# Token-major hashing with the bits in the split tile, in an attention and FFN kernel on one core

## The chip, the cores and the metric

The kernel runs on one core of one Trainium2 chip. The metric is the time of the kernel on the device in microseconds (us). Executions of the kernel before agree within 0.6% in four runs. The rounds ran on different chips. Each run has a state: "slow" if it took over 1.5% more than the fastest run of the same kernel.

TensorE has a clock that is granted to it, full or half.

## The reference, cut to what matters

Attention with a hash mask for 4 batches, 8 heads, 768 tokens and 64 dimensions a head, then an FFN with a maximum of three products:

```python
q_bits = (einsum('bhsd,dk->bhsk', q, proj) > 0)      # 6 bits; k_bits in the same way
mask = q_bucket[:, :, :, None] == k_bucket[:, :, None, :]
scores = where(mask, q @ k^T / 8, -1e9)
attn = softmax(scores);  x = (attn @ v) as [3072, 512]
h = maximum(maximum(x @ w1, x @ w2), x @ w3)
out = h @ w_out
```

## The kernel before

q and k are scaled and split into a high fp16 part (64 columns) and a rest (64 columns), in a tile `s` with tokens on the partitions, and transposed into `T`. The score matmul contracts 70 rows: 64 dimensions and 6 rows of hash bits, scaled so large that tokens of different buckets get no weight. Two heads form a pair, and half a sequence (384 tokens) of a pair is a block. A *unit* is one score tile of 256 keys by 384 queries: two score matmuls, one exponential on ScalarE, six attend matmuls two units later. There are 192 units, 12 per pair. The program is one hand-written order of steps, one step per unit; FFN matmul groups ("atoms") are strewn between the units once the first half of batch 0 is done.

The hash in the old kernel works on the transposed tile (bits by rows), with all tokens as moving columns, and writes the bits of each head into rows 64 to 69 of `T`:

```python
def hash_mm(sets):                          # 16 matmuls of 384 columns a pair
    for m, (i, w) in enumerate(ws):
        for g, (t, hh, half) in enumerate(sets[i]):
            nc.tensor.matmul(hps[32*g : 32*(g+1), 0:HQ], w[:], t[:, a : a + CH, :], ...)

def prep(b, pr, s):                         # batches 2 and 3, pr = 0..3
    ...                                     # (the high parts)
    at_end(s + 1, lambda: split_r("q", b, pr)); at_end(s + 1, lambda: xbar("q", b, pr))
    at_end(s + 3, lambda: split_r("k", b, pr)); at_end(s + 3, lambda: xbar("k", b, pr))
    tail(b, pr, s + 12)                     # the hash

for b in range(1, B):                       # (the steps of one pair; the next pair comes at s + 11)
        at(s - 8, lambda: load_pair(b, pr, nc.sync))
        (front if b == 1 else prep)(b, pr, s)
        at(s + 4, lambda: vcast(b, pr)); at(s + 9, lambda: meanv(b, pr), 0.34)
```

`xbar` is a transpose by DMA, put into the queue of SP, which also carries the loads of q, k, v and the outputs. (A transfer is *issued* when SP hands it over; it has *landed* when the profile shows its completion.) Batches 0 and 1 transpose on TensorE (`front`). Pairs follow each other by 11 steps, the loads of a pair go into the queue at step `s - 8`, and what stands in `at_end` goes in at the *end* of its step.

The softmax here doesn't subtract the row's maximum and nothing guards it: scores larger than these inputs give would overflow.

## Time and profile before

| | before |
|---|---|
| median time | 307.63 us (306.75 to 308.55, 4 runs) |
| span of the profile, mean granted clock | 306.0 us, 0.974 |
| score of unit 0, 35, 60, 132 starts at (TensorE's timeline) | 8.8, 56.8, 97.2, 200.2 us |
| first FFN matmul | 63.9 us |

How long a matmul really takes is read from start to next start in TensorE's timeline (start, length, what, and how many of them):

```profile
start us, us, engine line op out<-in xcount [idle before <-releaser]
190.77 0.49 PE L265 MATMUL sc<-qT,kT 70*128 70x384 f16 x2
191.10 0.35 PE L285 MATMUL av<-vone,AT 128*128 128x65 f16 x6
191.28 0.81 PE L329 MATMUL ps<-xT,w_sb 128*128 128x384 f16 x4
191.93 0.49 PE L265 MATMUL sc<-qT,kT 70*128 70x384 f16 x2
```

Two scores take 0.33 us (190.77 to 191.10), six attends 0.18 us, an FFN group 0.65 us.

What TensorE waits for most is VectorE (columns: us in all, times, longest):

```profile
PE tps L162 <- DVE qs L152: 11.9, 7, 4.3
```

### The profile page before, as it was taken

The numbers are of one execution on the slowest core, as the hardware profiler recorded it, in microseconds if no ns is written. First come the engines' busy times: TensorE is split into PE (matmuls) and PEld (weight loads), VectorE is DVE, ScalarE is ACT, GpSimd is POOL, SyncE is SP. The second block draws the span as 40 slices with busy tenths as digits, with TensorE's granted clock in tenths as the row PEclk, the third lists the DMA queues.
The fourth block names the chain that finished last, engine by engine and source line by source line (L and its number), as shares of the span: only waits on it lengthen the run. The fifth ranks groups of instructions, "written<-read, shape, count | busy, mean of one in ns | idle before, by whom it ended". The sixth has DMA issues, their size and how long they took to land.

```text
span 306.0 us, 7090 instructions
## 1 busy us (share of the span) xinstructions
PE 276.1 (90%) x2896; PEld 176.6 (58%) x2896; DVE 212.0 (69%) x455; ACT 200.6 (66%) x265; POOL 9.3 (3%) x17
## 2 busy tenths in 40 slices
PE   3847888989969989999999989999999999999994
PEld 1444565656646656565666556656666665666551
DVE  5687996877995867969587677969664454455551
ACT  3425658968646667777778676868676787786220
POOL 1370000000000000000000000000000000000000
PEclk9969979999997999999999999999999999999998
DMA  7999940006326285915809490926002001100202
GB/s 216 372 287 264 227 131 2 3 5 185 132 56 172 45 233 130 222 39 113 249 15 230 114 246 20 237 95 136 2 1 105 2 0 54 53 1 2 103 0 104
DMA packets 46080, 35.20 MB, mean 115 GB/s; under 512 B 26656, under 2 KB 42976, under 8 KB 46048
## 3 DMA queue, kind: packets, MB, share of 16 engines
q1 hardware_dynamic: 42016, 31.61, 37.7%
q0 software_dynamic: 3952, 3.15, 6.5%
q8 instruction: 22, 0.36, 0.5%
q14 instruction: 10, 0.08, 0.1%
q10 hardware_dynamic: 80, 0.00, 0.0%
HBM read 25.17 MB, written 6.29 MB: 103 GB/s over the span
## 4 chain that ended last, share of the span: by engine, by line
PE 74%; DVE 18%; ACT 3%; issue 2%; DMA 1%; SPq 0%; DVEq 0%; ACTq 0%
PE ps L329 28%; PE sc L265 16%; PE av L285 9%; PE po L341 9%; PE hps L179 4%; PE tps L162 4%; DVE qs L152 3%; ACT AT L269 2%; DVE hb L184 2%; DVE ks L146 2%; DVE ks L152 2%; PE xps L315 2%; DVE kT L188 2%; PE svp L244 1%; DVE t L301 1%
## 5 line engine op out<-in xcount | busy, mean ns | idle before, releaser
L269 ACT ACTIVATE AT<-sc,bias_t 128x768 f16<-128x768 f32 x192 | 169.1, 902 | 73.2 <-PE sc L265 72.7
L329 PE MATMUL ps<-xT,w_sb 128*128 128x384 f16 x576 | 112.4, 327 | 1.9 <-DVE ht L336 1.7
L265 PE MATMUL sc<-qT,kT 70*128 70x384 f16 x384 | 96.4, 332 | 4.2 <-ACT AT L269 1.6
L285 PEld LDWEIGHTS <-AT 128*128 128x128 f16 x1152 | 61.3, 98 | 31.1 <-issue 6.9
L336 DVE TENSOR_TENSOR ht<-ht,ps 128x384 f16<-128x384 f16 x96 | 52.9, 552 | 34.4 <-PE ps L329 31.6
L285 PE MATMUL av<-vone,AT 128*128 128x65 f16 x1152 | 67.1, 193 | 4.4 <-DVE t L301 4.3
L329 PEld LDWEIGHTS <-w_sb 128*128 128x128 f16 x576 | 50.8, 98 | 30.9 <-issue 5.8
L265 PEld LDWEIGHTS <-kT 70*128 70x128 f16 x384 | 34.0, 100 | 23.9 <-issue 6.4
L341 PE MATMUL po<-wout_sb,ht 128*128 128x512 f16 x144 | 34.8, 379 | 0.0
L334 ACT CAST ht<-ps 128x384 f16<-128x384 f32 x48 | 22.8, 474 | 16.3 <-PE ps L329 16.1
L301 DVE TENSOR_TENSOR t<-av,mv 128x390 f32<-128x390 f32 x32 | 17.9, 560 | 10.1 <-PE av L285 10.0
L184 DVE TENSOR_SCALAR hb<-hps 128x384 f16<-128x384 f32 x28 | 15.2, 553 | 8.7 <-PE hps L179 8.6
L162 PE MATMUL tps<-iden,qs 128*128 128x128 f16 x96 | 9.7, 259 | 12.7 <-DVE qs L152 11.9
L341 PEld LDWEIGHTS <-ht 128*128 128x128 f16 x144 | 12.8, 97 | 13.1 <-issue 0.6
L347 DVE COPY osb<-po 128x512 f32<-128x512 f32 x16 | 11.0, 688 | 11.5 <-PE po L341 11.5
L305 DVE TENSOR_TENSOR xn<-t,rr 128x384 f16<-128x384 f32 x32 | 17.9, 558 | 1.1
L152 DVE SCALAR_TENSOR_TENSOR qs<-q,qs 128x768 f16<-128x768 f32 (+1 forms) x17 | 16.5, 972 | 0.1
L162 PEld LDWEIGHTS <-qs 128*128 128x128 f16 x96 | 7.4, 116 | 14.7 <-DVE qs L152 13.3
L316 DVE COPY xT<-xps 128x384 f16<-128x384 f16 x32 | 11.3, 353 | 6.2 <-PE xps L315 5.9
L152 DVE SCALAR_TENSOR_TENSOR ks<-k,ks 128x768 f16<-128x768 f32 (+1 forms) x17 | 15.3, 906 | 0.3
L179 PE MATMUL hps<-kT,PA 128*32 128x384 f16 x64 | 11.1, 343 | 1.0 <-DVE kT L170 0.9
L170 DVE COPY kT<-tps 128x768 f16<-128x768 f16 x16 | 8.6, 553 | 4.3 <-PE tps L162 4.2
(43 smaller groups left out, 172.9 us busy)
## 6 DMA issues: line engine op xcount, KB each, us to landing
v<-in_v_dram SPq DMA_DIRECT2D x16, 384.0 KB
out_dram<-osb SPq DMA_DIRECT2D x24, 256.0 KB
q<-in_q_dram SPq DMA_DIRECT2D x15, 384.0 KB
k<-in_k_dram SPq DMA_DIRECT2D x15, 384.0 KB
w_sb<-in_moe_w_dram POOLq DMA_DIRECT2D x6, 384.0 KB, 13.3
wout_sb<-in_moe_w_out_dram POOLq DMA_DIRECT2D x1, 768.0 KB, 22.0
q<-in_q_dram SPq DMA_DIRECT2D x2, 192.0 KB
k<-in_k_dram SPq DMA_DIRECT2D x2, 192.0 KB
```

Of the source, the lines that this page charges most:

```text
L152: nc.vector.scalar_tensor_tensor(out=s[:, a, D : 2 * D], in0=x32, scalar=QS, in1=s[:, a, 0:D], op0=AluOp.mult, op1=AluOp.subtract)
L162: nc.tensor.transpose(p16[:, c * P : (c + 1) * P], S16[n, b, pr][:, hh * NCH + c, :], iden[:])
L179: nc.tensor.matmul(hps[32 * g : 32 * (g + 1), 0:HQ], w[:], t[:, a : a + CH, :], start=m == 0, stop=m == len(ws) - 1)
L184: nc.vector.tensor_scalar(out=out, in0=hps[:, 0:HQ], scalar1=0.0, scalar2=0.5, op0=AluOp.is_gt, op1=AluOp.subtract)
L265: nc.tensor.matmul(sc[:, i, 0:HQ], kT[0:KR, hh * NCH + 2 * j + i, :], qT[0:KR, hh * NCH + hf * CH : hh * NCH + (hf + 1) * CH, :], start=Tr ...
L269: nc.scalar.activation(AT[:], sc[:, :, 0:HQ], ActFn.Exp, bias=bias_t[:], scale=EXP_SCALE)
L285: nc.tensor.matmul(av[:, o : o + D + 1], AT[:, i, c * P : (c + 1) * P], vones[b % 2][:, 2 * pr + hh, 2 * j + i, 0 : D + 1], start=first, s ...
L301: nc.vector.tensor_tensor(out=t[:, :, :, 0 : D + 1], in0=av[:, :, :, 0 : D + 1], in1=mvs[b, pr][:].unsqueeze(2).to_broadcast([P, 2, CH, D ...
L329: nc.tensor.matmul(ps[:, 0:HQ], w_sb[i][:, jc, fb * P : (fb + 1) * P], xT[:, jc, :], start=jc == 0, stop=jc == NJ - 1)
L334: nc.scalar.copy(ht[:], ps[:, 0:HQ])
L336: nc.vector.tensor_tensor(out=hts[fb][:], in0=hts[fb][:], in1=ps[:, 0:HQ], op=AluOp.max)
L341: nc.tensor.matmul(ps[:], hts[fb][:, c * P : (c + 1) * P], wout_sb[:, fb, :], start=fb == 0, stop=fb == NF - 1)
```

## The change

The intent is to unload TensorE and VectorE. The hash becomes 24 matmuls of 12 columns a pair, with the transposed tokens as weights, so that the bits come out with tokens on the partitions. Three small VectorE operations write them into the split tile, over the rest part (which is not needed once the hash is made), and the tile is *transposed a second time*: now rows 64 to 69 of `T` hold the bits. x is transposed by DMA. V is summed on GpSimd, so that the mean of V takes one matmul, not six. In batch 0 half 0 of all pairs comes before half 1 of pair 1, so that the FFN can start after 35 units instead of 41. The start gets 32 matmuls to warm TensorE. Two more changes are not in the cut below: the preparation of a pair starts two steps earlier in batches 2 and 3 (three in batch 1), and the exponential takes its bias as a constant and no longer from a tile. The core of the diff (cuts marked):

```diff
+    def hash_bits(b, pr, heads=(0, 2)):
+        ... for n, hh, c:
+            nc.tensor.matmul(hps[:, a*2*NBITS : (a+1)*2*NBITS], T[b, pr][:, a, :], PAB[:], start=True, stop=True)
+        ... neg = -hps[6:12];  bit = hps[0:6] > neg;  s[:, :, D : D+NBITS] = (bit - 0.5) * 2*BIT
+    def T2(b, pr, s, by_pe):
+        at(s, lambda: hash_bits(b, pr), 0.7)
+        if by_pe: ... second transposes on TensorE (pairs 0 and 1 of batch 0)
+        else:
+            at_end(s, lambda: xbar("q", b, pr))
+            at_end(s, lambda: xbar("k", b, pr))
     def prep(b, pr, s):
         ... (first transposes by DMA, as before)
-        tail(b, pr, s + 12)
+        T2(b, pr, s + 9, False)
-    blocks = [... ((0, 0), (0, 1), (1, 0), (1, 1), (2, 0), (3, 0), (2, 1), (3, 1))]
+    blocks = [... ((0, 0), (0, 1), (1, 0), (2, 0), (3, 0), (1, 1), (2, 1), (3, 1))]
-            at(u + LAG + 3, lambda: x_T(b, hf, pr), 0.2)
+            ... first and last half: x_T as before; all others:
+                at(u + LAG + 2, lambda: x_bar(b, hf, pr))
+                if pr == NP - 1: at(u + LAG + 6, lambda: push_ffn(...))
+        nc.gpsimd.tensor_tensor(...)  x3   # V's sums, into one of two buffers vsums[pr % 2]
-            at(s + 9, lambda b=b, pr=pr: meanv(b, pr), 0.34)
+            at(s + 9, lambda b=b, pr=pr: meanv(b, pr), 0.06)
-    begin = 6 * NUP + 5
+    begin = 5 * NUP + 5
```

More of the change, by code (lines that the diff above doesn't have):

```diff
@@ L48 @@
     EPS = 1e-30
+    NA = 2 * 2 * NCH
+    NA2 = 2 * NCH
+    WARM = 32
     konst = ctx.enter_context(tc.tile_pool(name="konst", bufs=1))
     raw = ctx.enter_context(tc.tile_pool(name="raw", bufs=4))
-    spl = ctx.enter_context(tc.tile_pool(name="spl", bufs=3))
+    spl = ctx.enter_context(tc.tile_pool(name="spl", bufs=4))
     opnd = ctx.enter_context(tc.tile_pool(name="opnd", bufs=8))
@@ L88 @@
         load(n, 0, 1, nc.sync)
-    bias_t = konst.tile([P, 1], FP32, name="bias_t")
-    nc.vector.memset(bias_t[:], EXP_BIAS)
     warm = konst.tile([P, 1], FP32, name="warm")
-    nc.scalar.activation(warm[:], bias_t[:], ActFn.Exp)
+    nc.vector.memset(warm[:], 0.0)
+    nc.scalar.activation(warm[:], warm[:], ActFn.Exp)
+    ones = konst.tile([P, P], FP16, name="ones")
+    nc.vector.memset(ones[:], 1.0)
     iden = konst.tile([P, P], FP16, name="iden")
     make_identity(nc, iden[:])
-    ones = konst.tile([P, P], FP16, name="ones")
-    nc.vector.memset(ones[:], 1.0)
+    wps = mm_ps.tile([P, 512], FP32, tag="mm", name="wps")
+    for _ in range(WARM):
+        nc.tensor.matmul(wps[:, 0:P], ones[:], ones[:], start=True, stop=True)
+    vsums = []
+    for i in range(2):
+        t = konst.tile([P, 2, D + 1], FP16, name=f"vsum{i}", tag=f"vsum{i}")
+        nc.vector.memset(t[:, :, D : D + 1], float(NCH))
+        vsums.append(t)
     vones = []
@@ L102, with make_p @@
         vones.append(t)
-    ph = konst.tile([D, NBITS], FP16, name="ph")
-    pr32 = konst.tile([D, NBITS], FP32, name="pr32")
-    PA, PB = [], []
-    for i in range(2):
-        for n, l in (("PA", PA), ("PB", PB)):
-            l.append(konst.tile([P, 32], FP16, name=f"{n}{i}", tag=f"{n}{i}"))
-            nc.vector.memset(l[i][:], 0.0)
-    def make_p(i):
-        if i == 0:
-            nc.vector.tensor_copy(ph[:], p32[:])
-            nc.vector.tensor_tensor(out=pr32[:], in0=p32[:], in1=ph[:], op=AluOp.subtract)
+    PAB = konst.tile([P, 2 * NBITS], FP16, name="PAB")
+    def make_p():
+        ph = konst.tile([D, NBITS], FP16, name="ph")
+        pr32 = konst.tile([D, NBITS], FP32, name="pr32")
+        nc.vector.tensor_copy(ph[:], p32[:])
+        nc.vector.tensor_tensor(out=pr32[:], in0=p32[:], in1=ph[:], op=AluOp.subtract)
         for o in (0, D):
-            for l, src in ((PA, ph), (PB, pr32)):
-                nc.vector.tensor_scalar(out=l[i][o : o + D, NBITS * i : NBITS * (i + 1)], in0=src[:],
+            for i, src in enumerate((ph, pr32)):
+                nc.vector.tensor_scalar(out=PAB[o : o + D, NBITS * i : NBITS * (i + 1)], in0=src[:],
                                         scalar1=1024.0, scalar2=None, op0=AluOp.mult)
@@ L134, in operands, with chunks, raw_view @@
     def operands(b, pr):
-        for n in "qk":
-            S16[n, b, pr] = spl.tile([P, 2 * NCH, 2 * D], FP16, tag=n + "s", name=n + "s")
-            T[n, b, pr] = opnd.tile([P, 2 * NCH, P], FP16, tag=n + "T", name=n + "T")
+        S16[b, pr] = spl.tile([P, NA, 2 * D], FP16, tag="s", name="s")
+        T[b, pr] = opnd.tile([P, NA, P], FP16, tag="T", name="T")
+    def chunks(n, heads=(0, 2)):
+        o = NA2 * "qk".index(n)
+        return o + heads[0] * NCH, o + heads[1] * NCH
+    def raw_view(n, b, pr, heads):
+        return raws[n, b, pr][:].rearrange("p h (c d) -> p (h c) d", d=D)[:, heads[0] * NCH : heads[1] * NCH, :]
     def split_h(n, b, pr, eng, heads=(0, 2)):
-        a = slice(heads[0] * NCH, heads[1] * NCH)
-        x32 = raws[n, b, pr][:].rearrange("p h (c d) -> p (h c) d", d=D)[:, a, :]
-        o = S16[n, b, pr][:, a, 0:D]
+        a0, a1 = chunks(n, heads)
+        o = S16[b, pr][:, a0:a1, 0:D]
+        x32 = raw_view(n, b, pr, heads)
         if eng is nc.scalar:
@@ L148, in split_r @@
     def split_r(n, b, pr, heads=(0, 2)):
-        a = slice(heads[0] * NCH, heads[1] * NCH)
-        x32 = raws[n, b, pr][:].rearrange("p h (c d) -> p (h c) d", d=D)[:, a, :]
-        s = S16[n, b, pr]
-        nc.vector.scalar_tensor_tensor(out=s[:, a, D : 2 * D], in0=x32, scalar=QS,
-                                       in1=s[:, a, 0:D], op0=AluOp.mult, op1=AluOp.subtract)
+        a0, a1 = chunks(n, heads)
+        s = S16[b, pr]
+        nc.vector.scalar_tensor_tensor(out=s[:, a0:a1, D : 2 * D], in0=raw_view(n, b, pr, heads), scalar=QS,
+                                       in1=s[:, a0:a1, 0:D], op0=AluOp.mult, op1=AluOp.subtract)
     def xbar(n, b, pr):
-        nc.sync.dma_start_transpose(T[n, b, pr][:], S16[n, b, pr][:].rearrange("p a d -> p (a d)"))
+        a0, a1 = chunks(n)
+        nc.sync.dma_start_transpose(T[b, pr][:, a0:a1, :], S16[b, pr][:, a0:a1, :].rearrange("p a d -> p (a d)"))
     def pe_T(n, b, pr, hh):
@@ L160, in pe_T, with evac_T @@
         p16 = ps[:].bitcast(FP16)
+        a0, a1 = chunks(n, (hh, hh + 1))
         for c in range(NCH):
-            nc.tensor.transpose(p16[:, c * P : (c + 1) * P], S16[n, b, pr][:, hh * NCH + c, :], iden[:])
+            nc.tensor.transpose(p16[:, c * P : (c + 1) * P], S16[b, pr][:, a0 + c, :], iden[:])
         return p16
-    def evac_T(p16, n, b, pr, hh, eng, c0=0, c1=NCH):
-        o = T[n, b, pr][:, hh * NCH + c0 : hh * NCH + c1, :].rearrange("p a t -> p (a t)")
+    def evac_T(p16, n, b, pr, hh, eng):
+        a0, a1 = chunks(n, (hh, hh + 1))
+        o = T[b, pr][:, a0:a1, :].rearrange("p a t -> p (a t)")
@@ L167, in evac_T @@
         if eng is nc.scalar:
-            nc.scalar.copy(o, p16[:, c0 * P : c1 * P])
+            nc.scalar.copy(o, p16[:, 0 : NCH * P])
         else:
-            nc.vector.tensor_copy(o, p16[:, c0 * P : c1 * P])
-    def hash_mm(sets):
+            nc.vector.tensor_copy(o, p16[:, 0 : NCH * P])
+    def hash_bits(b, pr, heads=(0, 2)):
         hps = mm_ps.tile([P, 512], FP32, tag="mm", name="hps")
-        ws = [(i, l[i]) for l in (PA, PB) for i in range(len(sets))]
-        for m, (i, w) in enumerate(ws):
-            for g, (t, hh, half) in enumerate(sets[i]):
-                a = hh * NCH + half * CH
-                nc.tensor.matmul(hps[32 * g : 32 * (g + 1), 0:HQ], w[:], t[:, a : a + CH, :],
-                                 start=m == 0, stop=m == len(ws) - 1)
-        return hps
@@ L183, in hash_cmp @@
-    def hash_cmp(out, hps):
-        nc.vector.tensor_scalar(out=out, in0=hps[:, 0:HQ], scalar1=0.0, scalar2=0.5,
-                                op0=AluOp.is_gt, op1=AluOp.subtract)
-    def hash_row(dst, src):
-        nc.vector.tensor_scalar(out=dst, in0=src, scalar1=2 * BIT, scalar2=None, op0=AluOp.mult)
-    hbs = {}
-    def hash_pair(b, pr):
-        hb = small.tile([P, HQ], FP16, tag="hb", name="hb")
-        hbs[b, pr] = hb
-        g = [(T[n, b, pr], hh) for hh in range(2) for n in "qk"]
-        hash_cmp(hb[:], hash_mm([[(t, hh, half) for t, hh in g] for half in range(2)]))
-        hash_row(hb[:], hb[:])
@@ L199, in hash_half @@
-    def hash_half(b, pr, half):
-        if half == 0:
-            hbs[b, pr] = small.tile([P, S], FP16, tag="hb2", name="hb2")
-        g = [(T[n, b, pr], hh, half) for hh in range(2) for n in "qk"]
-        hash_cmp(hbs[b, pr][:, half * HQ : (half + 1) * HQ], hash_mm([g]))
-    def hash_head_rows(b, pr, hh):
-        for i, n in enumerate("qk"):
-            dst = T[n, b, pr][D : D + NBITS, hh * NCH : (hh + 1) * NCH, :].rearrange("p a t -> p (a t)")
-            o = 32 * (2 * hh + i)
-            hash_row(dst, hbs[b, pr][o : o + NBITS, :])
@@ L211, in hash_rows @@
-    def hash_rows(b, pr):
-        hb = hbs.pop((b, pr))
-        for g, (n, hh) in enumerate((("q", 0), ("k", 0), ("q", 1), ("k", 1))):
-            for half in range(2):
-                a = hh * NCH + half * CH
-                o = 32 * g + NBITS * half
-                nc.sync.dma_start(T[n, b, pr][D : D + NBITS, a : a + CH, :].rearrange("p a t -> p (a t)"),
-                                  hb[o : o + NBITS, :])
-    def hash_head(b, pr, hh):
-        tq, tk = T["q", b, pr], T["k", b, pr]
-        hb = small.tile([P, HQ], FP16, tag="hb", name="hb")
-        hash_cmp(hb[:], hash_mm([[(tk, hh, 0), (tq, hh, 0), (tk, hh, 1), (tq, hh, 1)]]))
-        for g, (t, half) in enumerate(((tk, 0), (tq, 0), (tk, 1), (tq, 1))):
-            a = hh * NCH + half * CH
-            hash_row(t[D : D + NBITS, a : a + CH, :].rearrange("p a t -> p (a t)"),
-                     hb[32 * g : 32 * g + NBITS, :])
+        for n in range(2):
+            for hh in range(*heads):
+                for c in range(NCH):
+                    a = n * NA2 + hh * NCH + c
+                    nc.tensor.matmul(hps[:, a * 2 * NBITS : (a + 1) * 2 * NBITS], T[b, pr][:, a, :], PAB[:],
+                                     start=True, stop=True)
@@ new lines, in hash_bits @@
+        bit = small.tile([P, 2, 2 * NCH, NBITS], FP16, tag="bit", name="bit")
+        hv = hps[:, 0 : NA * 2 * NBITS].rearrange("p (n a k) -> p n a k", n=2, k=2 * NBITS)
+        sl = slice(heads[0] * NCH, heads[1] * NCH)
+        neg = small.tile([P, 2, 2 * NCH, NBITS], FP32, tag="neg", name="neg")
+        nc.vector.tensor_scalar(out=neg[:, :, sl, :], in0=hv[:, :, sl, NBITS : 2 * NBITS], scalar1=-1.0,
+                                scalar2=None, op0=AluOp.mult)
+        nc.vector.tensor_tensor(out=bit[:, :, sl, :], in0=hv[:, :, sl, 0:NBITS], in1=neg[:, :, sl, :],
+                                op=AluOp.is_gt)
@@ L230, in vcast @@
+        s4 = S16[b, pr][:].rearrange("p (n a) d -> p n a d", n=2)
+        nc.vector.tensor_scalar(out=s4[:, :, sl, D : D + NBITS], in0=bit[:, :, sl, :], scalar1=0.5,
+                                scalar2=2 * BIT, op0=AluOp.subtract, op1=AluOp.mult)
+    mvs = {}
     def vcast(b, pr):
-        v32 = raws.pop(("v", b, pr))[:].rearrange("p h (c d) -> p h c d", d=D)
+        v32 = raws.pop(("v", b, pr))
         o = vones[b % 2][:, 2 * pr : 2 * pr + 2, :, 0:D]
+        src = v32[:].rearrange("p h (c d) -> p h c d", d=D)
@@ L233, in vcast @@
         if b == 0:
-            nc.gpsimd.tensor_copy(o, v32)
-        else:
-            nc.scalar.copy(o, v32)
-    mvs = {}
+            nc.gpsimd.tensor_copy(o, src)
+            return
+        nc.scalar.copy(o, src)
+        half = CH * D
+        t = small.tile([P, 2, half], FP32, tag="vt", name="vt")
+        nc.gpsimd.tensor_tensor(out=t[:], in0=v32[:, :, 0:half], in1=v32[:, :, half : 2 * half], op=AluOp.add)
+        t2 = small.tile([P, 2, D], FP32, tag="vt2", name="vt2")
+        nc.gpsimd.tensor_tensor(out=t2[:], in0=t[:, :, 0:D], in1=t[:, :, D : 2 * D], op=AluOp.add)
@@ L240, in meanv @@
+        nc.gpsimd.tensor_tensor(out=vsums[pr % 2][:, :, 0:D], in0=t2[:], in1=t[:, :, 2 * D : 3 * D], op=AluOp.add)
     def meanv(b, pr):
         ps = mm_ps.tile([P, 512], FP32, tag="mm", name="svp")
-        for c in range(NCH):
-            nc.tensor.matmul(ps[:, 0 : 2 * (D + 1)].rearrange("p (h d) -> p h d", h=2), ones[:],
-                             vones[b % 2][:, 2 * pr : 2 * pr + 2, c, 0 : D + 1], start=c == 0, stop=c == NCH - 1)
+        o = ps[:, 0 : 2 * (D + 1)].rearrange("p (h d) -> p h d", h=2)
@@ L246, in meanv @@
+        if b == 0:
+            for c in range(NCH):
+                nc.tensor.matmul(o, ones[:], vones[0][:, 2 * pr : 2 * pr + 2, c, 0 : D + 1],
+                                 start=c == 0, stop=c == NCH - 1)
+        else:
+            nc.tensor.matmul(o, ones[:], vsums[pr % 2][:], start=True, stop=True)
         mv = vpool.tile([P, 2, D + 1], FP32, tag=f"mv{pr}", name="mv")
@@ L252 @@
     NU = NCH // 2
-    blocks = [(0, hf, pr) for pr, hf in ((0, 0), (0, 1), (1, 0), (1, 1), (2, 0), (3, 0), (2, 1), (3, 1))]
+    blocks = [(0, hf, pr) for pr, hf in ((0, 0), (0, 1), (1, 0), (2, 0), (3, 0), (1, 1), (2, 1), (3, 1))]
     blocks += [(b, hf, pr) for b in range(1, B) for hf in range(2) for pr in range(NP)]
@@ L262, in score @@
         sc = sc_ps.tile([P, 2, 512], FP32, tag="sc", name="sc")
-        qT, kT = T["q", b, pr], T["k", b, pr]
+        qkT = T[b, pr]
         for i in range(2):
-            nc.tensor.matmul(sc[:, i, 0:HQ], kT[0:KR, hh * NCH + 2 * j + i, :],
-                             qT[0:KR, hh * NCH + hf * CH : hh * NCH + (hf + 1) * CH, :],
+            nc.tensor.matmul(sc[:, i, 0:HQ], qkT[0:KR, NA2 + hh * NCH + 2 * j + i, :],
+                             qkT[0:KR, hh * NCH + hf * CH : hh * NCH + (hf + 1) * CH, :],
                              start=True, stop=True)
         AT = atp.tile([P, 2, HQ], FP16, tag="AT", name="AT")
-        nc.scalar.activation(AT[:], sc[:, :, 0:HQ], ActFn.Exp, bias=bias_t[:], scale=EXP_SCALE)
+        nc.scalar.activation(AT[:], sc[:, :, 0:HQ], ActFn.Exp, bias=EXP_BIAS, scale=EXP_SCALE)
         ATs[u] = AT
@@ L289, in attend @@
             norm(b, hf, pr)
-            at(u + LAG + 3, lambda: x_T(b, hf, pr), 0.2)
+            if (b, hf) in ((0, 0), (B - 1, 1)):
+                at(u + LAG + 3, lambda: x_T(b, hf, pr), 0.2)
+            else:
+                at(u + LAG + 2, lambda: x_bar(b, hf, pr))
+                if pr == NP - 1:
+                    at(u + LAG + 6, lambda: push_ffn(b, hf, xTs.pop((b, hf))))
     xTs = {}
@@ L306, in norm, with x_tile, x_bar, x_T @@
                                 op=AluOp.mult)
-    def x_T(b, hf, pr):
+    def x_tile(b, hf):
         if (b, hf) not in xTs:
             xTs[b, hf] = xp.tile([P, NJ, HQ], FP16, tag="xT", name="xT")
+        return xTs[b, hf]
+    def x_bar(b, hf, pr):
+        o = x_tile(b, hf)[:, pr, :].rearrange("p (c t) -> p c t", c=CH)
+        nc.sync.dma_start_transpose(o, xns.pop((b, hf, pr))[:].rearrange("p c d -> p (c d)"))
+    def x_T(b, hf, pr):
+        x_tile(b, hf)
         xn = xns.pop((b, hf, pr))
@@ L368, in at_end, with tr, pair_T @@
         todo_end.setdefault(step, []).append(fn)
+    def tr(n, b, pr, hh, eng=nc.vector):
+        evac_T(pe_T(n, b, pr, hh), n, b, pr, hh, eng)
+    def pair_T(b, pr, hh, eng):
+        pq = pe_T("q", b, pr, hh)
+        pk = pe_T("k", b, pr, hh)
+        evac_T(pq, "q", b, pr, hh, nc.vector)
+        evac_T(pk, "k", b, pr, hh, eng)
     operands(0, 0)
@@ L375 @@
     split_r("k", 0, 0, (0, 1))
-    make_p(0)
-    pq = pe_T("q", 0, 0, 0)
-    pk = pe_T("k", 0, 0, 0)
-    evac_T(pq, "q", 0, 0, 0, nc.vector)
-    evac_T(pk, "k", 0, 0, 0, nc.vector)
+    pair_T(0, 0, 0, nc.scalar)
+    make_p()
     split_h("q", 0, 0, nc.scalar, (1, 2))
     split_h("k", 0, 0, nc.scalar, (1, 2))
+    hash_bits(0, 0, (0, 1))
+    pair_T(0, 0, 0, nc.scalar)
     split_r("q", 0, 0, (1, 2))
-    hash_head(0, 0, 0)
     split_r("k", 0, 0, (1, 2))
@@ L388, in first_b @@
     def first_b():
-        pq = pe_T("q", 0, 0, 1)
-        pk = pe_T("k", 0, 0, 1)
-        evac_T(pq, "q", 0, 0, 1, nc.vector)
-        evac_T(pk, "k", 0, 0, 1, nc.vector)
+        pair_T(0, 0, 1, nc.vector)
+        hash_bits(0, 0, (1, 2))
+        pair_T(0, 0, 1, nc.vector)
     at(1, first_b)
-    at(2, lambda: hash_head(0, 0, 1))
     def load_pair(b, pr, eng):
@@ L399, in load_pair, with front @@
             load(n, b, pr, eng)
-    def front(b, pr, s):
+    def T2(b, pr, s, by_pe):
+        at(s, lambda: hash_bits(b, pr), 0.7)
+        if by_pe:
+            at(s + 1, lambda: pair_T(b, pr, 0, nc.vector), 0.7)
+            at(s + 2, lambda: pair_T(b, pr, 1, nc.vector), 0.7)
+        else:
+            at_end(s, lambda: xbar("q", b, pr))
+            at_end(s, lambda: xbar("k", b, pr))
+    def front(b, pr, s, by_pe=False):
         at(s, lambda: operands(b, pr))
@@ L407, in front @@
         at_end(s + 1, lambda: split_r("k", b, pr))
-        def tr(n, hh):
-            evac_T(pe_T(n, b, pr, hh), n, b, pr, hh, nc.vector)
+        k = 2 if b == 0 else 1
         for i, (n, hh) in enumerate((("q", 0), ("q", 1), ("k", 0), ("k", 1))):
-            at(s + 2 + i // (2 if b == 0 else 1), lambda n=n, hh=hh: tr(n, hh), 0.34)
-        tail(b, pr, s + (4 if b == 0 else 7))
-    def tail(b, pr, s):
-        if b == 1:
-            at(s, lambda: hash_pair(b, pr), 0.67)
-            at(s, lambda: hash_rows(b, pr))
-        else:
-            at(s, lambda: hash_half(b, pr, 0), 0.34)
-            at(s + (b > 0), lambda: hash_half(b, pr, 1), 0.34)
-            for hh in range(2):
-                at_end(s + (b > 0) * (1 + hh), lambda hh=hh: hash_head_rows(b, pr, hh))
-    at(0, lambda: vcast(0, 1))
-    at(0, lambda: load_pair(0, 2, nc.sync))
-    at(2, lambda: make_p(1))
-    front(0, 1, 2)
-    at(2, lambda: meanv(0, 0), 0.34)
-    at(3, lambda: load_pair(0, 3, nc.sync))
-    at(6, lambda: vcast(0, 2))
-    for i in range(3):
-        at(7 + i, lambda i=i: load_w(i, 0))
-        at(15 + i, lambda i=i: load_w(i, 1))
-    front(0, 2, 11)
-    at(10, lambda: meanv(0, 1), 0.34)
-    at(15, lambda: vcast(0, 3))
-    front(0, 3, 18)
-    at(20, lambda: meanv(0, 2), 0.34)
-    at(26, lambda: meanv(0, 3), 0.34)
-    at(18, lambda: nc.gpsimd.dma_start(wout_sb[:], moe_w_out.rearrange("(c p) m -> p c m", p=P)))
+            at(s + 2 + i // k, lambda n=n, hh=hh: tr(n, b, pr, hh), 0.34)
+        T2(b, pr, s + 2 + 4 // k, by_pe)
     def prep(b, pr, s):
@@ L451, in prep @@
         at_end(s + 3, lambda: xbar("k", b, pr))
-        tail(b, pr, s + 12)
+        T2(b, pr, s + 9, False)
+    at(0, lambda: vcast(0, 1))
+    at(0, lambda: load_pair(0, 2, nc.sync))
+    at(1, lambda: load_pair(0, 3, nc.sync))
+    front(0, 1, 2, True)
+    at(3, lambda: meanv(0, 0), 0.34)
+    at(5, lambda: vcast(0, 2))
+    for i in range(3):
+        at(4 + i, lambda i=i: load_w(i, 0))
+        at(9 + i, lambda i=i: load_w(i, 1))
+    front(0, 2, 8)
+    at(10, lambda: meanv(0, 1), 0.34)
+    at(12, lambda: vcast(0, 3))
+    front(0, 3, 13)
+    at(17, lambda: meanv(0, 2), 0.34)
+    at(22, lambda: meanv(0, 3), 0.34)
+    at(16, lambda: nc.gpsimd.dma_start(wout_sb[:], moe_w_out.rearrange("(c p) m -> p c m", p=P)))
     for b in range(1, B):
         for pr in range(NP):
-            s = 33 + 7 * pr if b == 1 else 2 * (b - 1) * NUG + 4 + 11 * pr
+            s = 30 + 7 * pr if b == 1 else 2 * (b - 1) * NUG + 2 + 11 * pr
             at(s - 8, lambda b=b, pr=pr: load_pair(b, pr, nc.sync))
```

## The prediction

> **What bounds the kernel now.** From about 100 us to the end, TensorE: in the table of busy time by stretches of 10 us, PE is busy 9.2 to 10.0 of 10 us from 100 to 300 us, and VectorE falls to 5 to 7. From 10 to 60 us it is the preparation of the first pairs on VectorE (busy 7 to 9 of 10 us) together with the chains PE-VectorE-PE of hashing; ScalarE's exponentials, 192 of 0.90 us, wait for scores there (in the timeline score unit 5 runs at 21.9, unit 23 at 47.7, unit 41 at 64 us: 1.3 us a unit where the exponential needs 0.85). The FFN starts at 63.9 us. The last 20 us are a TensorE tail (FFN of the last half) and an output DMA, and don't change.
>
> **TensorE's real cost, by start-to-start times in PE's timeline (190 to 200 us).** Two scores 0.33, six attends 0.18 (30 ns each), an FFN group 0.65, an output group 1.29, three x transposes 0.17, six mean-V matmuls 0.35, hashing half a pair about 0.45 with its gaps (0.85 a pair). Sum about 259 us, so 47 us are idle or throttled: 4 at the start, 4 to 5 at the end, most of the rest before 130 us.
>
> **What the change does on TensorE.** Hashing becomes 24 matmuls of 12 columns with 128-column weights. At the attend rate of 30 ns they take 0.7 us a pair: little saved, about 0.15 x 16 = 2.4 us. (The Trainium skill, "TensorE: Matmul & The Clock Gate", Back-to-back issue gap, gives about 25 ns as the floor for small matmuls; the 30 ns agree roughly.) Mean V: 12 x 0.29 = 3.5 us saved. x transposes to DMA: 24 x 0.17 = 4.1 us saved. Second transposes of two pairs: 2.7 us added, where TensorE is idle anyway. So about 10 us leave the TensorE-bound part, all critical.
>
> **VectorE.** Hash compare and rows, 2.5 us a pair, become three small operations, about 0.7 us. 24 evictions of 0.35 us go. Pairs 0 and 1 get four more evictions of 0.55 us each. Before the FFN VectorE has some 5 us less, but the start chain is longer: a second transpose round, make_p behind the first eviction; +1 us to the first score, +2 us for head 1.
>
> **Order.** The FFN can start after 35 units instead of 41. With 1.3 us a unit and less VectorE work I expect its first matmul at 57 us instead of 63.9. That lets 157 instead of 151 units be mixed with FFN.
>
> **DMA.** A 384 KB transpose takes some 3.3 us from issue, 2 us of it at 210 GB/s (stretches of 0.5 us at 206 to 210 us; the skill, "DMA: Bandwidth & Descriptors", Latency and other measured facts, states 261 GB/s, the trace shows less). Second transposes in steady state have slack; pair 2 and 3 of batch 0 have 6 to 7 units, beside weight loads: 1 to 3 us of stall. The eight small row DMAs a pair of batch 1 (0.73 us of issue each) go.
>
> **Sum.** 57 + 218 (TensorE work left) + 10 (stalls, 12 now) + 4.5 (end) = 290 us; I say 291. Range 284 to 299. Chances: faster 0.87, same 0.11, slower 0.02.
>
> **Right or wrong if the profile shows:** FFN's first matmul at 54 to 60 us; hash matmuls 25 to 32 ns apart; TensorE 10 of 10 us from 110 us on; VectorE busy down by 25 to 30 us in all.
>
> **What would make it wrong:** transposes queueing behind loads and output on SP, so that FFN groups or scores wait for xT or T; GpSimd's sums slowing VectorE (weight issues stretch a 0.95 us operation to 2.09 at 17.6 us); hash matmuls limited by weight loads at 60 ns or more.

## More of the kernel before

From the page of the kernel before: busy time of TensorE, then busy tenths of TensorE in 40 slices of the span, its granted clock, and the busy share of the 16 DMA engines.

```profile
PE 276.1 (90%) x2896; PEld 176.6 (58%) x2896; DVE 212.0 (69%) x455; ACT 200.6 (66%) x265; POOL 9.3 (3%) x17
...
PE   3847888989969989999999989999999999999994
...
PEclk9969979999997999999999999999999999999998
DMA  7999940006326285915809490926002001100202
```

The next view gives busy time of each engine in three stretches, and at the end of each line the granted clock, the DMA share and GB/s.

```profile
core 0: us, PE busy (x) PEld busy (x) DVE busy (x) ACT busy (x) POOL busy (x), PEclk, DMA share, GB/s
96.00:126.00 30.00, 28.99 (x326) 18.20 (x324) 22.43 (x48) 21.61 (x29) 0.00 (x0) 1.00 0.60 147
126.00:160.00 34.00, 33.55 (x351) 20.78 (x349) 25.68 (x56) 25.60 (x34) 0.00 (x0) 1.00 0.47 126
160.00:210.00 50.00, 48.94 (x513) 30.31 (x511) 37.64 (x79) 37.11 (x51) 0.00 (x0) 1.00 0.71 159
```

From 126 us TensorE is busy all the time, and the DMA engines 0.47 to 0.71 of it.

The queue of SP around one k transpose looks like this (start, time of issue, what):

```profile
122.47 1.43 SPq L156 DMA_TRANSPOSE qT<-qs  x1
123.95 0.89 SPq L78 DMA_DIRECT2D q<-in_q_dram  x1
124.89 0.47 SPq L78 DMA_DIRECT2D k<-in_k_dram  x1
125.41 0.47 SPq L78 DMA_DIRECT2D v<-in_v_dram  x1
126.30 1.69 SPq L156 DMA_TRANSPOSE kT<-ks  x1
```

The k transpose is issued behind the three loads of the next pair. The loads cost it no time in the queue here: VectorE's last operation on its data ended at 126.3 us too. Its hash comes nine steps later, and no wait of TensorE for a transpose by DMA stands in the list of waits.

## The result, and the profile after

The changed kernel took 328.38 us in the median (325.75 to 330.95, 4 runs), against 307.63. The ratio is 1.063 (1.055 to 1.071). Ratios here and below are the mean time of one kernel's fast runs over that of the other's in the same rounds, so they are not quite the ratio of the medians quoted. The profiled run, 330.95 us, counts as slow; the three fast ones had a clock of 0.909 to 0.911, the profiled one 0.895.

The same lines of the page, after:

```profile
PE 288.7 (88%) x2972; PEld 190.8 (58%) x2972; DVE 191.5 (58%) x398; ACT 189.1 (57%) x267; POOL 35.3 (11%) x53
...
PE   6697797979779885959999995979999999999795
...
PEclk9559876789997997896999997895999999999999
DMA  7999469658569997585895987598563003001102
```

TensorE's row has holes, the clock row has many more low digits, and the DMA row is fuller. By stretches, with the columns as before:

```profile
96.00:126.00 30.00, 23.38 (x266) 15.43 (x265) 18.78 (x38) 16.86 (x24) 5.36 (x8) 0.94 1.04 224
126.00:160.00 34.00, 29.53 (x257) 17.64 (x258) 17.24 (x36) 17.22 (x25) 2.74 (x5) 0.80 0.67 147
160.00:210.00 50.00, 46.02 (x485) 29.72 (x483) 27.93 (x60) 32.85 (x48) 5.72 (x9) 0.93 0.86 189
```

From 96 to 126 us the DMA share is 1.04, against 0.60 (packets count where they start, so a share can come out slightly above 1; I read it as: the engines are full). TensorE's clock falls to 0.80 from 126 to 160 us. The waits of TensorE name what it stands for:

```profile
engine line waited for: us in total, times, longest us
PE hps L190 <- DMA T<-s: 12.9, 5, 4.6
PE tps L173 <- DVE s L161: 5.8, 6, 1.9
...
PE sc L250 <- DMA T<-s: 1.9, 1, 1.9
```

The hash matmuls, of which none waited for the DMA before, wait 12.9 us. For a second transpose a score waits only once, before unit 24, the first of pair 3 of batch 0 (at 51.7 us). One of the stops at the hash, in TensorE's timeline:

```profile
121.94 0.45 PE L190 MATMUL hps<-PAB,T 128*128 128x12 f16 x12
126.95 0.49 PE L190 MATMUL hps<-PAB,T 128*128 128x12 f16 x12 [4.56 <-DMA T<-s]
127.29 0.27 PE L230 MATMUL svp<-vsum,ones 128*128 128x130 f16 x1
127.35 0.84 PE L250 MATMUL sc<-T 70*128 70x384 f16 x2
127.99 0.54 PE L270 MATMUL av<-vone,AT 128*128 128x65 f16 x6
```

The hash of q runs at 121.94, and that of k has to wait 4.56 us for its first transpose. Then the same two scores take 0.64 us (127.35 to 127.99) that took 0.33: half clock. Why the transpose is late stands in the queue of SP:

```profile
117.29 1.39 SPq L305 DMA_TRANSPOSE xT<-xn  x1
118.73 0.59 SPq L81 DMA_DIRECT2D q<-in_q_dram  x1
119.36 0.47 SPq L81 DMA_DIRECT2D k<-in_k_dram  x1
119.92 0.41 SPq L81 DMA_DIRECT2D v<-in_v_dram  x1
120.44 0.41 SPq L347 DMA_DIRECT2D out_dram<-osb  x1
120.94 3.34 SPq L166 DMA_TRANSPOSE T<-s  x1
```

The data of this k transpose were complete at 116.7 us (the end of VectorE's rest operation of k in the trace). The queue first issued an x transpose, the three loads of the next pair (1.2 MB) and an output; the k transpose was issued at 120.94, 4.2 us late, and landed at 126.9, behind the loads, which landed at 122.7 to 124.8.

To see where the time went, each matmul's time to the next matmul's start was compared with the usual spacing of its form at full clock. What was more is "idle" where TensorE had ended for over 0.1 us, and "half clock" where the granted clock was half; this is worked out from the traces, and is good to perhaps 1 us. "Half clock" in us is thus what it cost, and not how long it lasted. The first column is the time to unit 60, then follow units 60 to 132 with their idle and half-clock parts, and the rest.

| profile | to unit 60 | units 60 to 132 | of it idle | of it half clock | unit 132 to end |
|---|---|---|---|---|---|
| before | 97.2 | 103.0 | 2.5 | 0.0 | 105.7 |
| changed | 108.2 | 119.2 | 14.0 | 11.2 | 101.8 |
| changed, loads behind (e9 below) | 100.9 | 101.9 | 5.3 | 2.7 | 102.5 |
| same, later hash, old order (e10 below) | 102.2 | 96.5 | 1.4 | 0.0 | 103.5 |

The stretches don't hold quite the same FFN work: up to unit 60 the old kernel does 14 FFN groups of 0.65 us, e10 15, and the changed kernel and e9, with the new order, 18; from unit 132 it is 72, 70, 69 and 69, and the last three have two output groups of 1.29 us less there. So a first or last column is comparable between the kernels only to within 2 to 5 us. And up to step 42 the changed kernel and e9 are the same program: most of the 7.3 us between their first columns is the start, which varies from run to run (unit 35 came at 57.3 to 64.4 us with the same instructions).

### The profile page after: what moved, and what is told of

It is laid out like the page before. It is cut to its first block, busy times and chain, and to the rows that moved or that the text cites. A ratio compares the mean times of both kernels' runs of the same rounds, so it can differ in the third digit from the quotient of the medians.

```text
span 329.2 us, 7303 instructions
## 1 busy us (share of the span) xinstructions
PE 288.7 (88%) x2972; PEld 190.8 (58%) x2972; DVE 191.5 (58%) x398; ACT 189.1 (57%) x267; POOL 35.3 (11%) x53
## 4 chain that ended last, share of the span: by engine, by line
PE 66%; DVE 15%; DMA 13%; ACT 2%; issue 2%; SPq 1%; ACTq 0%; DVEq 0%
PE ps L327 27%; PE sc L250 15%; DMA T<-s 11%; PE av L270 8%; PE po L339 8%; PE tps L173 4%; DVE s L161 4%; PE hps L190 2%; DVE s L156 2%; ACT AT L254 2%; DMA xT<-xn 2%; DVE T L182 1%; DVE ht L334 1%; DVE xn L295 1%; DVE t L291 1%
## 5 line engine op out<-in xcount | busy, mean ns | idle before, releaser
L254 ACT ACTIVATE AT<-sc 128x768 f16<-128x768 f32 x192 | 153.0, 811 | 99.6 <-PE sc L250 97.7
L250 PE MATMUL sc<-T 70*128 70x384 f16 x384 | 104.8, 358 | 3.6 <-DMA T<-s 1.9
L270 PEld LDWEIGHTS <-AT 128*128 128x128 f16 x1152 | 66.0, 103 | 34.9 <-issue 12.9
L250 PEld LDWEIGHTS <-T 70*128 70x128 f16 x384 | 35.0, 105 | 21.4 <-issue 4.5
L173 PE MATMUL tps<-iden,s 128*128 128x128 f16 x240 | 24.2, 262 | 9.9 <-DVE s L161 5.8
L216 POOL TENSOR_TENSOR vt<-v 128x384 f32<-128x384 f32 x12 | 11.9, 995 | 154.4 <-DMA v<-in_v_dram 154.4
L182 DVE COPY T<-tps 128x768 f16<-128x768 f16 x38 | 20.3, 552 | 10.7 <-PE tps L173 10.2
L190 PE MATMUL hps<-PAB,T 128*128 128x12 f16 x384 | 13.5, 170 | 14.8 <-DMA T<-s 12.9
L173 PEld LDWEIGHTS <-s 128*128 128x128 f16 x240 | 19.1, 120 | 12.9 <-DVE s L161 7.9
L190 PEld LDWEIGHTS <-T 128*128 128x128 f16 x384 | 11.9, 98 | 16.3 <-DMA T<-s 13.4
L161 DVE SCALAR_TENSOR_TENSOR s<-q,s 128x768 f16<-128x768 f32 (+1 forms) x17 | 17.0, 1004 | 0.2
```

The costliest lines, as they stand in the source:

```text
L161: nc.vector.scalar_tensor_tensor(out=s[:, a0:a1, D : 2 * D], in0=raw_view(n, b, pr, heads), scalar=QS, in1=s[:, a0:a1, 0:D], op0=AluOp.mul ...
L173: nc.tensor.transpose(p16[:, c * P : (c + 1) * P], S16[b, pr][:, a0 + c, :], iden[:])
L182: nc.vector.tensor_copy(o, p16[:, 0 : NCH * P])
L190: nc.tensor.matmul(hps[:, a * 2 * NBITS : (a + 1) * 2 * NBITS], T[b, pr][:, a, :], PAB[:], start=True, stop=True)
L250: nc.tensor.matmul(sc[:, i, 0:HQ], qkT[0:KR, NA2 + hh * NCH + 2 * j + i, :], qkT[0:KR, hh * NCH + hf * CH : hh * NCH + (hf + 1) * CH, :], ...
L254: nc.scalar.activation(AT[:], sc[:, :, 0:HQ], ActFn.Exp, bias=EXP_BIAS, scale=EXP_SCALE)
```

## The experiments

Four kernels of the second group were sent twice, since no chip ran them the first time; they carry a "b". All results are correct but those of e12 and e14.

### e1: the hash three steps later

```diff
-        T2(b, pr, s + 9, False)
+        T2(b, pr, s + 12, False)
```

> The changed kernel, with only the hash (and so the second transpose) of the pairs of batch 2 and 3 moved from step s+9 to s+12, 9 steps after the k transpose is put in the queue, as the old kernel had it. Theory 1 (too little time between the first transpose by DMA and its hash; TensorE stops 3.5 to 4.6 us three times at the hash and then runs at half clock for 6.8 us each time): the waits of hash matmuls for DMA fall from 12.9 us to under 2 us, the granted clock rises, and the time falls by 18 to 26 us to 302 to 310 us. Rival (the DMA engines are full in this stage): the wait moves to the second transpose or stays; the time stays above 320 us.

Measured: 315.38 us, ratio 1.022 (1.018 to 1.026). It lies between what the two theories expected. TensorE still waits for transposes at the hash:

```profile
PE hps L190 <- DMA T<-s: 8.5, 3, 4.8
```

The DMA share was 0.93 to 1.00 from 96 to 210 us. In one pair the k data were ready at 111.3 us, the transpose was issued at 118.2 and landed at 126.0. So time for the transpose is worth 13 us, but it is not the whole cause.

### e2: idle matmuls in the place of three stops

```diff
+        fill = {(2, 1): 72, (2, 2): 60, (3, 1): 60}.get((b, pr), 0)
         for n in range(2):
+            for _ in range(fill * n):
+                nc.tensor.matmul(hps[:, 384:512], ones[:], ones[:], start=True, stop=True)
```

> The changed kernel, with 72, 60 and 60 idle matmuls of 128 columns (about 4.0, 3.4 and 3.4 us at 56 ns) put between the q and the k part of the hash of the three pairs where TensorE had stopped 4.56, 3.52 and 3.65 us for the k transpose. They do no useful work and use the wait. Theory (the stop itself takes the clock down): the clock stays 1.0 after these three hashes, and the time falls by about 3 x 3.4 = 10 us (6.8 us at half clock each) to about 318 us. Rival (the clock falls for another reason, or only follows the hash's small matmuls): half clock stays there and the time stays within 3 us of 328.

Measured: 322.94 us, ratio 1.046 (1.041 to 1.050), 5 us less than the changed kernel, not 10. Behind the second and third of these hashes the clock stayed full; at the first a stop of 3.00 us was left and half clock lasted for 3.4 us instead of 6.8. In units 60 to 132 the cost of half clock fell from 11.2 to 3.2 us and idle from 14.0 to 7.1, while 10.7 us of idle matmuls were added. So the stops do take the clock down, and that costs nearly as much as the stops. Where TensorE multiplied in the meantime, even uselessly, the kernel was faster.

### e3: x transposed on TensorE again

```diff
-            if (b, hf) in ((0, 0), (B - 1, 1)):
+            if True:
```

> The changed kernel with all x transposes back on TensorE, as the old kernel had them; nothing else is undone. This takes 24 DMA transposes of 1.2 to 1.7 us of issue out of the SP queue. If the SP queue's order and length is what makes the k transpose late (its data were ready at 116.7 us and it was issued at 120.9): hash waits fall by half or more, the time falls by 5 to 15 us though TensorE does 4 us more. If the x transposes are innocent: the time rises by 4 us.

Measured: 319.56 us, ratio 1.033 (1.028 to 1.039): 9 us less. But the hash waits did not fall, they were 13.5 us; what fell is the half clock (5.2 us in units 60 to 132). So the time came as the first theory said and the waits did not. In the trace the k data of batches 2 and 3 landed 7.2 us after they were ready, against 7.4 us in the changed kernel: the x transposes are not what makes the k transpose late.

### e4: V's sums alone, in the old kernel

The diff is that of `vcast`, `meanv` and `vsums` above, on the kernel before.

> The old kernel with only V's sums on GpSimd and one mean-V matmul instead of six for batches 1 to 3. If the term of the prediction holds: 3.5 us less than before (about 304 us, ratio 0.989). Rival (GpSimd's sums slow VectorE or come late): no gain, or slower.

Measured: 311.39 us, ratio 1.005 (0.998 to 1.013): no gain. In the profile units 60 to 132 and the rest each took 1.7 us less, as the removed matmuls promise, but units 35 to 60 took 4.4 us more. TensorE stopped twice for a mean of V:

```profile
PE ps L345 <- DVE mv L263: 3.7, 2, 2.0
```

In the changed kernel the same stop is seen from GpSimd. There are two buffers for the sums; a sum waits until the mean of two pairs before has been read (13.51 us, at the end of the first line below), and everything behind it is late. These are GpSimd's lines in its timeline of the changed kernel at that time, and then a line of VectorE's timeline beside them:

```profile
94.66 1.06 POOL L219 TENSOR_TENSOR vsum<-vt,vt 128x128 f16<-128x128 f32 x1 [13.51 <-PE svp L230]
95.68 0.99 POOL L216 TENSOR_TENSOR vt<-v 128x384 f32<-128x384 f32 x1
96.75 1.05 POOL L218 TENSOR_TENSOR vt<-vt 128x128 f32<-128x128 f32 x1
```
```profile
95.78 1.70 DVE L161 SCALAR_TENSOR_TENSOR s<-k,s 128x768 f16<-128x768 f32 x1
```

The VectorE operation took 1.70 us where its median is 0.95; the second and third GpSimd operations ran at the same time. The Trainium skill, "GPSIMD Engine Reference", Specifications, says that GpSimd's interfaces to SBUF are shared with VectorE, with contention for instructions with two SBUF inputs; this one has two, and the trace agrees. Over the whole trace the lengthened operations add up to 5.2 us, against 2.5 us in the old kernel (excess over each form's median, where it is over 0.05 us); all 12 of them, and all 6 in the old kernel, ran while GpSimd was busy. That is small beside the rest.

### e5b: later hash, and loads behind the k transpose

```diff
-            at(s - 8, lambda b=b, pr=pr: load_pair(b, pr, nc.sync))
+            at(s - (8 if b == 1 else 7), lambda b=b, pr=pr: load_pair(b, pr, nc.sync))
-        T2(b, pr, s + 9, False)
+        T2(b, pr, s + 12, False)
```

> The first experiment (hash at s+12) and, in addition, the loads of the next pair put in the queue one step later for batches 2 and 3, so that they come behind the k transpose and not in front of it (1.2 MB in front of it: in the first experiment the k transpose was issued at 118.2 us and landed 7.8 us later, behind three loads and an output). Theory of order: the k transpose lands 4 us sooner, hash waits fall from 8.5 us to under 2 us, time 304 to 308 us. Rival, the DMA engines are full (share 0.93 to 1.00 from 96 to 210 us in the first experiment, against 0.47 to 0.71 in the old kernel): whatever comes last waits; the time stays at 312 us or more, the share near 1.

Measured: 304.94 us, ratio 0.986 (0.977 to 0.996). In its profiled run, which is a slow one (309.99 us), no hash waited for a transpose any more, while the DMA share stayed at 0.91 to 1.05 from 96 to 210 us. The engines are full in both; what counts is which transfer comes last. The theory of order held, and its rival fell.

### e6b: the first transposes on TensorE

```diff
-            (front if b == 1 else prep)(b, pr, s)
+            front(b, pr, s)
```

> The changed kernel with the first transposes of batches 2 and 3 on TensorE, as in batch 1; the second ones stay on the DMA. TensorE gets 8 x 24 transposes of 56 ns more, 10.8 us, VectorE 8 x 4 evictions of 0.55 us; the DMA loses 16 of its 44 transposes of 384 KB. If the full DMA is what stops TensorE: no hash waits for DMA, DMA share from 96 to 210 us about 0.7, clock 1.0 there; time 328 less 13 us of waits, less some 12 us of half clock, plus 11 us: 312 to 318 us. Rival (TensorE alone bounds this stage and the stops are made up for later): about 11 us slower than 328.

Measured: 318.24 us, ratio 1.032 (1.024 to 1.039), just above the 312 to 318 us expected. There were no waits of hash for DMA, the DMA share was 0.55 to 0.62 from 126 to 210 us, and the clock was full there. It buys off the stops with TensorE's and VectorE's time, and is worse than waiting in the right order.

### e7b and e8b: the old hash with the three other parts, and the block order alone

e7b is the old kernel with V's sums, x by DMA and the new block order; e8b has the block order alone (`blocks` and `begin` of the diff).

> The old kernel, its hash and its preparation unchanged, with the three other parts: V's sums on GpSimd, x transposed by DMA, and the new block order with the FFN's start at unit 35. If the second transpose of the hash is what costs the time, this one is faster than the old kernel: 4 us from x, up to 3.5 us from V (the run with V alone gained 1.8 us behind unit 132 and lost 4 us at two late means), 2 to 4 us from the order: 298 to 304 us. Rival (the order or the x transposes on DMA cost it): slower than 310 us.

> The old kernel with only the block order changed (half 0 of all pairs first in batch 0, FFN from unit 35). The prediction counted 6 more units that can be mixed with FFN. If it holds: 2 to 5 us less. Rival (VectorE can't prepare pair 3 for unit 24 as it must now instead of unit 30): same or slower, with scores waiting for pair 2 and 3 before unit 30.

Measured: e7b 310.38 us, ratio 1.005 (0.995 to 1.014); e8b 312.99 us, ratio 1.016 (1.008 to 1.024). The new order alone costs 5 us in the old kernel. Unit 30 starts at 56.5 us, against 52.6, and a score waits 1.00 us for VectorE at 50.8 us. The FFN starts 1.8 us earlier, not 7. The median of e7b lies at the rival's bound of 310 us, but its ratio shows no difference: these three parts don't by themselves cost the 6%, nor do they gain what was expected. Its units 35 to 60 took 6.9 us more, of which four FFN groups (2.6 us) are work that came earlier, with stops of 1.99 and 1.91 us at means of V and half clock after them. The stretch from unit 132 took 3.2 us less, with four FFN groups and two output groups (5.2 us) less in it.

### e9: loads behind the k transpose, nothing else

The first edit of e5b alone.

> The changed kernel with only the loads of batches 2 and 3 put one step later, behind the k transpose; the hash stays at s+9. It completes the square of hash place and load place: 328 us as given, 315.4 with the later hash, 304.9 with both. If the place of the loads in the queue is the main thing, this one alone gains most: 308 to 314 us, hash waits under 6 us. If the two only work together (the transpose needs the 9 steps and the free queue): 317 to 324 us.

Measured: 307.91 us, ratio 1.002 (0.995 to 1.009). One constant, 8 to 7 for two batches, is worth 20 us of the 328: with it the changed kernel equals the old one. Its profiled run is a fast one. In the traces 16.6 us of the gain lie behind unit 60. The queue around a k transpose:

```profile
114.17 1.48 SPq L166 DMA_TRANSPOSE T<-s  x1
115.71 0.86 SPq L81 DMA_DIRECT2D q<-in_q_dram  x1
116.62 0.47 SPq L81 DMA_DIRECT2D k<-in_k_dram  x1
117.19 0.41 SPq L81 DMA_DIRECT2D v<-in_v_dram  x1
```

The k transpose was put in before the loads; it landed at 117.9 us, 3.7 us after its issue. (The data had been ready since 109.4 us: the queue was still late, by 4.8 us.) Over the eight pairs of batches 2 and 3 the k data landed 5.4 us after they were ready, against 7.4 us in the changed kernel (means of the differences in the traces). From ready to issue it was 1.4 us against 1.7, from issue to landing 4.0 against 5.7. So the new place mostly shortens the time under way, in which the loads' data had been in front, and less the wait for the issue. TensorE's wait at the hash:

```profile
PE hps L190 <- DMA T<-s: 5.2, 3, 2.9
```

### e10: e5b with the old block order

```diff
+    (e5b, and blocks and begin as in the kernel before)
```

> The changed kernel with later hash and loads behind (304.9 us) and, in addition, the old block order with the FFN from unit 41. The old kernel with the new order alone was 1.6% slower. If the order costs as much here: 298 to 302 us, and no wait of scores for the second transposes of pairs 2 and 3 in batch 0 (1.8 us at 51 us). Rival (with its cheaper VectorE work the changed kernel gains from the order): 305 us or more.

Measured: 302.87 us, ratio 0.987 (0.979 to 0.995). The ratio is that of e5b, so in the changed kernel the order makes no difference that these runs can show, though no score waits for pairs 2 and 3 any more. The hash wait is nearly gone:

```profile
PE hps L190 <- DMA T<-s: 0.9, 1, 0.9
```

### e11: four sum buffers and a later FFN

```diff
-    for i in range(2):          # vsums; vsums[pr % 2] becomes vsums[pr]
+    for i in range(NP):
-                    at(u + LAG + 6, lambda: push_ffn(b, hf, xTs.pop((b, hf))))
+                    at(u + LAG + 8, lambda: push_ffn(b, hf, xTs.pop((b, hf))))
```

> As the run before, with two more repairs: four buffers instead of two for V's sums (GpSimd waited 13.5 us for a buffer, which held TensorE 2.05 us at a mean V at about 97 us), and the FFN of a half starts two steps later after its last x transpose (TensorE waited 1.1 to 3.2 us for xT at about 203 us). If both waits are on the chain: 2 to 5 us under the run before, 294 to 299 us. If not: the same time.

Measured: 303.83 us, ratio 0.987 (0.980 to 0.994). No gain. In its profiled run, a slow one (309.73 us), the stop at a mean of V is 1.05 us instead of 2.06, but other waits for VectorE grew. A wait for xT stands neither in this list of waits nor in that of e10, so that repair had nothing left to mend; the two waits were not what sets the time.

### e12, e13 and e14: what holds the start?

e12 adds five idle matmuls after each attend of units 0 to 34 to e10; e14 does the same to the old kernel; e13 has the second transposes of pairs 2 and 3 of batch 0 on TensorE in e10 (`front(0, 2, 8, True)`, `front(0, 3, 13, True)`).

```diff
+        if u < 35 and not (hh == 1 and j == NU - 1):
+            for _ in range(5):
+                nc.tensor.matmul(av[:, 400:512], ones[:], ones[:, 0:112], start=True, stop=True, ...)
```

> The version with later hash, loads behind and old block order (302.9 us) with five idle matmuls of 112 columns[...] after each attend of the first 35 units, where TensorE has time to spare (useful work 34 of 59 us). Theory (in the start the changed kernel loses to the half clock: profiled starts with the same instructions took 57.3 to 64.4 us to unit 35, with 5.5 to 15 us lost to the half clock): half clock in units 0 to 35 falls by half or more, time 298 to 301 us, with less spread. Rival (the start is bound by VectorE and the chain of two transposes, the clock matters little): same time or up to 5 us slower.

> The same base (302.9 us) with the second transposes of pairs 2 and 3 of batch 0 on TensorE too, not on the DMA. VectorE gets 8 evictions of 0.55 us more. If the DMA round trip of these two pairs holds the start: 1 to 3 us faster. If VectorE bounds the start: 3 to 5 us slower.

> The old kernel with the same five idle matmuls after each attend of the first 35 units, nothing else. If the half clock of the start is a cost of its own in both kernels: 1 to 3 us faster than the old kernel (it lost some 4 to 7 us to half clock before unit 35). If idle matmuls only take time: up to 3 us slower.

e12 and e14 give a wrong result: these matmuls were written into the bank in which attend accumulates, and the results differ from there on. The amount of work is the same, so their times are used, with that reserve. e12: 303.45 us, ratio 0.983 (0.976 to 0.990). The cost of half clock before unit 35 went from 8.6 us to none, but unit 35 started at 58.3 us instead of 59.0. At unit 60 its profile is 3.9 us ahead of e10's (98.3 against 102.2), of which 2.8 us are lost again behind it. e14: 311.39 us, ratio 1.010 (1.001 to 1.019), barely slower. e13: 304.24 us, ratio 0.988 (0.982 to 0.994), no difference. So neither the half clock nor the DMA round trip in batch 0 holds the first 35 units by itself. What does is open. It was only argued, not shown, that the longer chain from TensorE to VectorE and back, now passed twice, does.

## Why the prediction was wrong

- **What bounds the kernel, and TensorE's savings: right.** The 24 hash matmuls of a pair start 25 ns apart: this line gives (0.75 - 0.17) / 23, where 0.17 us is the length of one.

```profile
66.13 0.75 PE L190 MATMUL hps<-PAB,T 128*128 128x12 f16 x24
```

  (The Trainium skill, "TensorE: Matmul & The Clock Gate", Back-to-back issue gap, states a floor of about 25 ns; the trace agrees.) About 10 us were to leave TensorE's part. In e10 units 60 to the end take 200.0 us against 208.7, with the same FFN work but for one group of 0.65 us: 8.7 us came, once the waits were gone.
- **"Second transposes in steady state have slack": this step failed, as the account of the DMA path.** Of the *second* transposes it was true: none was waited for in steady state, and the 1 to 3 us of stall forecast for pairs 2 and 3 of batch 0 were 1.86 us. But the prediction took this for the whole cost, and the *first* transpose had lost slack: its hash moved from s+12 to s+9, and it sat behind 1.2 MB of loads in a queue that now also carried the second transposes and x. The prediction looked at one transpose of 3.3 us and did not add up what the queue carries: the DMA share from 96 to 126 us went from 0.60 to 1.04. The k data needed up to 10 us from ready to landed, TensorE waited 12.9 us for them at the hash, and half clock followed. That this is the cause is shown by e9, which changes the place of the loads and nothing else and takes back 20 us by the medians (19 by the ratios). The prediction named queueing on SP as a risk, but for FFN groups and scores, and gave slower 2 chances in 100.
- **The clock: a term that was missing.** The sum had a row for stalls (10 us, where "12 now" were counted) and none for what a stop does to the clock. Units 60 to 132 lost 11.5 us more to idle time than before, and 11.2 us more to half clock. e2 shows, at two of three hashes, that it is the stops that bring it. The Trainium skill, "TensorE: Matmul & The Clock Gate", Part 1, gives a window of about 3.4 us by which the clock is judged; the half-clock stretches in the traces last 3.413 or 6.827 us, or longer multiples (but for those cut off by a trace's end), which agrees.
- **"I expect its first matmul at 57 us": wrong in the profiled run, uncertain in others.** It came at 65.0 us; in e9, which is the same up to there, at 58.1 us. The two differ in what half clock cost before unit 35 (15.2 and 5.5 us). The first score came 1.0 us later and the first of head 1 (unit 3) 3.0 us later, 17.2 against 14.2, where 1 and 2 were expected.
- **The order: wrong.** "That lets 157 instead of 151 units be mixed with FFN" was counted as gain. Alone it made the old kernel 1.6% slower, and in the changed kernel it made no difference (e5b and e10).
- **VectorE down by 25 to 30 us: nearly.** It went from 212.0 to 191.5 us, 20.5 us less. Of the missing part 2.7 us (5.2 less 2.5) are operations that were lengthened while GpSimd worked.
- **The sum.** Of the 37 us between 328 and 291, 20 are the place of the loads (e9) and, by the ratios 1.002 and 0.986, some 5 the place of the hash; the intervals of these two ratios touch. Some 12 are left. In e10 the first 60 units took 5 us more than in the old kernel, where the prediction had counted on less. Half clock may be a good part of it, as e12 without it until unit 35 is only 1.1 us behind the old kernel at unit 60; but e12's time did not fall clear of noise, so the start is not explained.

e5b, e10, e11 and e13, which give correct results, beat the old kernel by 1.2 to 1.4%, with intervals below 1. None is clearly over 2%.

## What to carry to other kernels

When a transfer moves onto a queue that already works, write down everything that the queue carries between the moment when the data are ready and the moment when they are needed, in order; a transfer that somebody waits for belongs in front of one that nobody needs for ten microseconds. A stop of TensorE costs its own length and, here, nearly as much again at half clock (14.0 and 11.2 us in units 60 to 132). When a change moves a step nearer to what it depends on (here s+12 to s+9), look for the slack that the old distance had hidden.

## What the Trainium skill lacked or had wrong

- "DMA: Bandwidth & Descriptors", Latency and other measured facts, gives 261 GB/s for DMA transposes with a non-contiguous middle dimension, and more for contiguous ones. Here the DMA engines moved 207 to 217 GB/s with only a transpose under way (five stretches of 0.5 us, at 208.0 to 209.5 and 212.0 to 213.0 us of the kernel before), at a DMA share above 1. The page has no time of issue for a transpose of this size on this chip: it was 1.3 to 3.3 us for 384 KB, against 0.4 to 1.0 us for most loads. Nor has it one from issue to landing: 3.6 us at least, 4.0 in the median, 7.5 at most (44 transposes of the changed kernel).
- "TensorE: Matmul & The Clock Gate", HAM oscillation, sums up its rule as no idle gaps over about 3.4 us, and the page gives no length for the short idle times that it names in a second case. In the kernel before a stop of 1.05 us, ending at 41.5 us, came with a stretch of 3.4 us at half clock; TensorE had been busy for 2.44 of the 3.42 us before it. A stop of 1.86 us in the changed kernel, ending at 51.7 us, was followed by 10.2 us of it. TensorE was not stopped in these 10 us, but worked at scores, attends and a few transposes.
